# Linear attention beside a gated mixer, one core: a different tiling of the matrix M, and new places for den and r

## The chip, the cores and the metric

The kernel runs on one core of a Trainium2 chip. Times are device microseconds (us) of whole executions. A profiled execution also has a span, from its first to its last instruction, which is about 2 us shorter than the time.

The engines are named as in the profile: PE is TensorE's matmuls, PEld its weight loads, DVE VectorE, ACT ScalarE, POOL GpSimd, SP the sync engine that issues the DMAs. A `q` after a name is the engine's own instruction queue.

## The reference

The input is `x` of 2048 x 640 (bf16). Two branches are mixed by a gate per row.

```python
# A: linear attention, 32 heads of 20
q, k, v = split(x @ wqkv)                      # each [32, 2048, 20]
pq, pk = phi(q), phi(k)                        # phi(t) = (t+1 if t>0 else exp(t)) + 1e-6
kv  = einsum("hsd,hse->hde", pk, v)
z   = pk.sum(over s)
den = einsum("hqd,hd->hq", pq, z) + 1e-6
a   = (einsum("hqd,hde->hqe", pq, kv) / den) @ wo
# B: mixer
h  = gelu(layernorm(x) @ w1);  hs = shift_rows_of_four_column_groups(h) @ w2
x1 = x + hs
b  = x1 + gelu(layernorm(x1) @ w3) @ w4
out = g * a + (1 - g) * b                      # g = sigmoid((x * gate_w).sum(-1))
```

The kernel uses three rearrangements. It forms G = pk^T x first and then kv = G wv, so that v is never formed. It folds the block-diagonal kv into `wo` as one 640 x 640 matrix M, so that the attention branch is (pq / den) M. The reciprocals r = 1/den are spread over the features by four small matmuls (`r_unit`) and multiplied into pq (`scale_t`). The feature axis of q, k and M is stored in five chunks `j` of 128 rows, each row being (head, part i of 4).

## The kernel before

Only the parts that the change and the argument touch are shown; `pair()` hands out one of four PSUM buffers of two banks each, which is all of PSUM.

```python
    ps = ctx.enter_context(tc.tile_pool(name="ps", bufs=4, space=PSUM))
    def pair():
        return ps.tile([P, 2, 512], F32, name="pp")
    ...
    def den_mm():                       # four column groups of 32, one per tile of 512 rows
        pt = pair()
        for j in range(DC):
            for t in range(NT):
                nc.tensor.matmul(pt[32*t:32*(t+1), 0, :], lhsT=zbd[:, j, :], rhs=pqT[:, j, t*TS:(t+1)*TS], ...)
    def den_evac(pt):
        nc.scalar.activation(pt[:, 1, :], pt[:, 0, :], ACT.Copy, bias=1e-6)
        nc.vector.reciprocal(r_bf[:], pt[:, 1, :])
    def r_unit():                       # four row groups of 32
        pts = [pair(), pair()]
        for t in range(NT):
            nc.tensor.matmul(pts[t//2][:, t%2, :], lhsT=emat[32*t:32*(t+1), :], rhs=r_bf[32*t:32*(t+1), :], ...)
        for k in range(2):
            nc.scalar.copy(rb[:, 2*k:2*k+2, :], pts[k][:])
    ...
    def kv_unit():                      # six groups of up to 6 heads: 25 matmuls of 120 columns, 5 of 40
        ...                             # then 8 masked copies on DVE into kvT
    def m_unit(j):                      # 2 halves x 2 parts x 4 column groups
        pt = pair()
        for hf in range(2):
            for p in range(2):
                for q in range(4):
                    g = pairs_qg[2*q + p][1]
                    nc.tensor.matmul(pt[32*q:32*(q+1), hf, 0:HD], lhsT=kvT[:, 2*q + p, j, :],
                                     rhs=wo_sb[:, g, hf*HD:(hf+1)*HD], start=(p == 0), stop=(p == 1))
        nc.scalar.copy(m_sb[:, j, :].rearrange("p (h e) -> p h e", h=2), pt[:, :, 0:HD])
    ...
    for fcs in w1_split: w1_unit(0, fcs)        # W1 of tile 0, in three units: (0,1), (2,3), (4,)
    kv_unit()
    den_evac(den_mm())
    for cc in range(CPT): ln1_apply(3*CPT + cc)
    for fcs in w1_split: w1_unit(1, fcs)        # W1 of tile 1
    for j in range(DC): m_unit(j)
    r_unit()
    # then W2 of tile 0, W1 of tiles 2 and 3, and per tile W3, attention, W4
```

Of the kernel before, what the change touches and what calls it, by code (L numbers as in the profile page):

```python
# [7 lines left out]
ACT = mybir.ActivationFunctionType  # L8
# [8 lines left out]
def kernel(  # L17
# [14 lines left out]
    P = 128  # L32
# [12 lines left out]
    CG = D // 4  # L45
    shifts = [1, -1, 2, -2]
    YMAX = 60.0
    GH = 6
    GW = GH * Dh
    NG = 6  # L50
    row0 = [g * GW for g in range(5)] + [D - P]
    head0 = [g * GH for g in range(6)]
    heads = [min(GH, H - h) for h in head0]

    x2 = A_x.rearrange("b s d -> (b s) d")
    out2 = out.rearrange("b s d -> (b s) d")
# [12 lines left out]
    def pair():  # L69
        return ps.tile([P, 2, 512], F32, name="pp")  # L70
# [6 lines left out]
    w1x = const.tile([P, DC, P], BF16)  # L77
    w2_sb = const.tile([P, DC, D], BF16)
    w3_sb = const.tile([P, DC, F], BF16)
    wo_sb = const.tile([P, NG, D], BF16)  # L80
    m_sb = const.tile([P, DC, D], BF16)
    pairs_qg = [(0, 0), (0, 1), (1, 1), (1, 2), (2, 2), (2, 3), (3, 4), (3, 5)]
    kvT = const.tile([P, len(pairs_qg), DC, 32], BF16)
    rb = const.tile([P, NT, TS], BF16)
    r_bf = const.tile([P, TS], BF16)
    ident = const.tile([P, P], BF16)
# [2 lines left out]
    hmask = const.tile([P, H], F32)  # L89
    zbd = const.tile([P, DC, H], BF16)  # L90
    emat = const.tile([P, P], BF16)
    bmask = const.tile([P, GH * 4], F32)
    bmask5 = const.tile([P, 8], F32)
    ylog = const.tile([P, NCH], F32)
    gate = const.tile([P, NCH], F32)
    omg = const.tile([P, NCH], F32)
# [11 lines left out]
    gT = wk_sb  # L108
    xT = st1.tile([P, DC, S], BF16)
    pk = st1.tile([P, NCH, D], BF16)  # L110
    gs = st1.tile([P, 2, D], BF16)
    e_p = s1.enter_context(tc.tile_pool(name="e_p", bufs=3))

# [23 lines left out]
    load_x(8, 12)  # L137
    load_x(12, 16)
    sp.dma_start(wv_sb[:], wqkv_v[:, :, 2 * D:3 * D])
    sp.dma_start(w1_sb[:], B_w1.rearrange("(c p) f -> p c f", p=P))  # L140
    for g in range(NG):
        sp.dma_start(wo_sb[:, g, :], A_wo[row0[g]:row0[g] + P, :])
    for g in range(4):
        sp.dma_start(w2_sb[:, g, :], B_w2[CG * g:CG * g + P, :])
        sp.dma_start(w2_sb[32 * g:32 * (g + 1), 4, :], B_w2[CG * g + P:CG * (g + 1), :])
# [14 lines left out]
    for t in range(4):  # L160
# [2 lines left out]
                                base=0, pattern=[[1, P]], channel_multiplier=-4)  # L163
        nc.gpsimd.affine_select(out=sl, in_=sl, compare_op=ALU.is_ge, fill=0.0,
                                base=3, pattern=[[-1, P]], channel_multiplier=4)
    for m, n, off in ((bmask, GH, 0), (bmask5, 2, 88)):
        nc.gpsimd.memset(m[:], 1.0)
        nc.gpsimd.affine_select(out=m[:], in_=m[:], compare_op=ALU.is_ge, fill=0.0,
                                base=-off, pattern=[[-Dh, n], [0, 4]], channel_multiplier=1)
        nc.gpsimd.affine_select(out=m[:], in_=m[:], compare_op=ALU.is_ge, fill=0.0,  # L170
                                base=off + Dh - 1, pattern=[[Dh, n], [0, 4]], channel_multiplier=-1)
    nc.gpsimd.memset(kvT[:], 0.0)
    for g in range(4):
        nc.gpsimd.tensor_copy(w1x[:, :, 32 * g:32 * (g + 1)], w1_sb[:, :, CG * g + P:CG * (g + 1)])

# [24 lines left out]
    def warmup(n, w=TS):  # L200
        for i in range(n):
            nc.tensor.matmul(warm[:, 1, 0:w], lhsT=one[:, 0:P], rhs=one[:, 0:w], start=True, stop=True)

    warmup(6)
    warmup(3, P)
    kp = pair()
    turns = [(pair()[:, 0, :].bitcast(BF16), a, b) for a, b in ((0, 2), (2, DC))]
    tg = warm[:, 0, :].bitcast(BF16)
    for n, (ptb, a, b) in enumerate(turns):
# [3 lines left out]
        if n == 0:  # L213
            nc.tensor.transpose(tg[:, 0:DC], g5[:], ident[0:DC, 0:DC])
            nc.vector.tensor_copy(wk_sb[:, :, D], tg[:, 0:DC])
    warmup(3, P)
    for dc in range(DC):
        k_mm(kp, 0, (dc,))
        if dc < DC - 1:
# [23 lines left out]
    def den_mm():  # L243
# [3 lines that stand above are left out]
                nc.tensor.matmul(pt[32 * t:32 * (t + 1), 0, :], lhsT=zbd[:, j, :], rhs=pqT[:, j, t * TS:(t + 1) * TS],  # L247
                                 start=(j == 0), stop=(j == DC - 1))
        return pt

    def den_evac(pt):
        nc.scalar.activation(pt[:, 1, :], pt[:, 0, :], ACT.Copy, bias=1e-6)
        with nc.allow_low_precision(reason="rounded after a float32 division, as a copy would"):
            nc.vector.reciprocal(r_bf[:], pt[:, 1, :])

    def r_unit():
        pts = [pair(), pair()]
        for t in range(NT):
            nc.tensor.matmul(pts[t // 2][:, t % 2, :], lhsT=emat[32 * t:32 * (t + 1), :],
                             rhs=r_bf[32 * t:32 * (t + 1), :], start=True, stop=True)  # L260
        for k in range(2):
            nc.scalar.copy(rb[:, 2 * k:2 * k + 2, :], pts[k][:])

    def scale_t(t):
        sl = pqT[:, :, t * TS:(t + 1) * TS]
        nc.vector.tensor_tensor(sl, sl, rb[:, t:t + 1, :].broadcast_to([P, DC, TS]), op=ALU.mult)
# [69 lines left out]
    def w1_unit(t, fcs):  # L336
        pt = pair()
        for i, fc in enumerate(fcs):
            for dc in range(DC):
                w = w1_sb[:, dc, CG * fc:CG * fc + P] if fc < 4 else w1x[:, dc, :]  # L340
                nc.tensor.matmul(pt[:, i, :], lhsT=w, rhs=lnxT[t][:, dc, :], start=(dc == 0), stop=(dc == DC - 1))  # L341
        for i, fc in enumerate(fcs):
            if fc < 4:
                o = 2 + shifts[fc] + t * TS
                nc.scalar.activation(hsT[:, fc, o:o + TS], pt[:, i, :], ACT.Gelu_apprx_tanh)
            else:
                hx = hx_p.tile([P, TS], BF16, name="hx")
                nc.scalar.activation(hx[:], pt[:, i, :], ACT.Gelu_apprx_tanh)
                for g in range(4):
                    o = 2 + shifts[g] + t * TS  # L350
                    nc.vector.tensor_copy(hsT[32 * g:32 * (g + 1), 4, o:o + TS], hx[32 * g:32 * (g + 1), :])
# [2 lines left out]

    def kv_unit():
        pt = pair()
        for g in range(NG):
            n = heads[g] * Dh
            for fc in range(DC):
                nc.tensor.matmul(pt[:, g // 3, (g % 3) * GW:(g % 3) * GW + n], lhsT=wv_sb[:, fc, row0[g]:row0[g] + P],  # L360
                                 rhs=gT[:, fc, 0:D].rearrange("p (j h i) -> p j h i", j=DC, h=H)
                                 [:, :, head0[g]:head0[g] + heads[g], :], start=(fc == 0), stop=(fc == DC - 1))
        for b, (q, g) in enumerate(pairs_qg):
            h0, h1 = max(8 * q, head0[g]), min(8 * q + 8, head0[g] + heads[g])
            a0, a1 = h0 - head0[g], h1 - head0[g]
            m = bmask5 if g == 5 else bmask
            base = (g % 3) * GW
            nc.vector.tensor_tensor(
                kvT[:, b, :, 4 * (h0 - 8 * q):4 * (h1 - 8 * q)],
                pt[:, g // 3, base:base + heads[g] * Dh].rearrange("p (j a) -> p j a", j=DC)[:, :, 4 * a0:4 * a1],  # L370
                m[:, 4 * a0:4 * a1].unsqueeze(1).broadcast_to([P, DC, 4 * (a1 - a0)]), op=ALU.mult)

    def m_unit(j):
        pt = pair()
        for hf in range(2):
            for p in range(2):
                for q in range(4):
                    g = pairs_qg[2 * q + p][1]
                    nc.tensor.matmul(pt[32 * q:32 * (q + 1), hf, 0:HD], lhsT=kvT[:, 2 * q + p, j, :],  # L379
                                     rhs=wo_sb[:, g, hf * HD:(hf + 1) * HD], start=(p == 0), stop=(p == 1))  # L380
        nc.scalar.copy(m_sb[:, j, :].rearrange("p (h e) -> p h e", h=2), pt[:, :, 0:HD])  # L381

    nc.gpsimd.memset(hsT[:, :, 0:4], 0.0)
    nc.gpsimd.memset(hsT[:, :, S:S + 4], 0.0)
    for fcs in w1_split:
        w1_unit(0, fcs)
    kv_unit()
    den_evac(den_mm())
    for cc in range(CPT):
        ln1_apply(3 * CPT + cc)  # L390
    for fcs in w1_split:
        w1_unit(1, fcs)
    s1.close()
    w4p = ctx.enter_context(tc.tile_pool(name="w4p", bufs=1))
    w4_sb = w4p.tile([P, FF + 1, D], BF16)
# [1 line left out]
    x1p = ctx.enter_context(tc.tile_pool(name="x1p", bufs=8))  # L397
    st = {}

    for j in range(DC):  # L400
        m_unit(j)
    r_unit()


    def w2_unit(t, cc):
        c = t * CPT + cc
        if cc == 0:
            st[t] = dict(x1=[], mv=small.tile([P, CPT, 2], F32, name="mv2"))
        pt = pair()
        for hf in range(2):  # L410
            for fc in range(DC):
                nc.tensor.matmul(pt[:, hf, 0:HD], lhsT=hsT[:, fc, 2 + c * P:2 + (c + 1) * P],  # L412
                                 rhs=w2_sb[:, fc, hf * HD:(hf + 1) * HD], start=(fc == 0), stop=(fc == DC - 1))
        x1 = x1p.tile([P, D], F32, name="x1")
        nc.vector.tensor_tensor(x1[:].rearrange("p (h e) -> p h e", h=2), pt[:, :, 0:HD],  # L415
                                x_sb[:, c, 0:D].rearrange("p (h e) -> p h e", h=2), op=ALU.add)
        ln_stats(st[t]["mv"][:, cc, :], x1[:], small.tile([P, 2, 6], F32, name="bnst")[:])
        st[t]["x1"].append(x1)

    def ln2_rstd(t, c0, c1):  # L420
        if c0 == 0:
            st[t]["rstd"] = small.tile([P, CPT], F32, name="rstd2")
        rsqrt(st[t]["rstd"][:, c0:c1], st[t]["mv"][:, c0:c1, 1])
# [102 lines left out]

    for cc in range(CPT):
        w2_unit(0, cc)
        ln2_rstd(0, cc, cc + 1)
        if cc >= 1:  # L530
            ln2_apply(0, cc - 1)
# [4 lines left out]
    nc.sync.dma_start(w4_sb[:, 0:FF, :], B_w4[0:FF * P, :].rearrange("(c p) f -> p c f", p=P))  # L536
    nc.sync.dma_start(w4_sb[0:FR, FF, :], B_w4[FF * P:F, :])
    nc.sync.dma_start(w4_sb[FR:P, FF, :], B_w4[FF * P:F, :])
    scale_t(0)
    scale_t(1)  # L540
    for fcs in w1_split:
# [48 lines left out]
```

## Time and profile before

| | before |
|---|---|
| time, median of 3 first runs (range) | 266.99 us (266.32 to 267.23) |
| span of the profiled run | 265.1 us |
| PE busy | 259.4 us, 98% of the span |
| granted TensorE clock (1 is full speed) | 0.997 |

Two lines from the head of the page of the kernel before: the span, then per engine the busy microseconds, their share of the span and the number of instructions.

```profile
span 265.1 us, 4244 instructions
PE 259.4 (98%) x1728; PEld 162.0 (61%) x1744; DVE 139.3 (53%) x270; ACT 84.2 (32%) x122; POOL 20.3 (8%) x55
```

PE hardly ever stops, so what shortens PE's work or one of its few waits shortens the kernel. The stretch that the change rebuilds is best read from the chain of waits (start, length, engine, tile, line of the kernel, number of instructions). L360 is kv, L247 den, L379 M, L381 the copies of M out of PSUM, L412 W2, L459 W3. W1 (tile 1 between den and M, tiles 2 and 3 between W2 and W3) is left out.

```profile
1.78 3.93 DMA wk_sb<-in_A_wqkv_dram
...
76.73 1.43 PE pp L360 x30
78.16 1.19 PE pp L247 x20
...
84.86 0.69 PE pp L379 x16
85.56 2.49 ACT m_sb L381 x4
88.10 5.59 PE pp L412 x40
...
104.48 0.22 PE pp L459
```

From kv's start (76.73) to W3's start (104.48) takes 27.75 us. I use this stretch, "kv to W3", throughout: no DMA from outside starts or ends it. W2 waits for four ScalarE copies of M. The timeline of the kernel before shows how tightly:

```profile
84.78 2.90 PE L379 MATMUL pp<-wo_sb,kvT 128*32 128x320 bf16 x80
85.56 3.08 ACT L381 CAST m_sb<-pp 128x640 bf16<-128x640 f32 x5
87.62 0.40 PE L259 MATMUL pp<-r_bf,emat 32*128 32x512 bf16 x4
87.94 5.41 PEld L412 LDWEIGHTS <-hsT 128*128 128x128 bf16 x40 [0.23 <-issue]
88.10 5.59 PE L412 MATMUL pp<-w_sb,hsT 128*128 128x320 bf16 x40
```

M keeps PE to about 87.6 and r to about 87.9. W2's weights are in at 87.94, but its first matmul needs a PSUM pair that the fourth copy frees, and starts at 88.10. So at most 0.16 us of PE is lost there. The reciprocal, 3.36 us on DVE from 80.07 on, runs beside W1 and costs nothing.

### The profile page before, as it was taken

Reading aid. Unit: us, or ns where it says so; the run is one execution under the profiler, and the core shown is the slowest. Engines: PE = TensorE matmul, PEld = TensorE weight load, DVE = VectorE, ACT = ScalarE, POOL = GpSimd, SP = SyncE. Lnnn points to the kernel's source line nnn. Section 1 sums busy time; section 2 is a strip of 40 time slices with the busy share of each in tenths; the row PEclk is TensorE's granted clock in tenths of the full one; section 3 lists DMA queues with packets and bytes.
Section 4 is the critical chain, followed back from the end, with each engine's and each line's share of the span. In section 5 each row is a group of like instructions: output and inputs, shape, how many; then the busy total and the mean of one; then the engine's idle time right before and its main releaser. Section 6 shows DMA issues by size and latency. Waiting matters only on the chain.

```text
span 265.1 us, 4244 instructions
## 1 busy us (share of the span) xinstructions
PE 259.4 (98%) x1728; PEld 162.0 (61%) x1744; DVE 139.3 (53%) x270; ACT 84.2 (32%) x122; POOL 20.3 (8%) x55
## 2 busy tenths in 40 slices
PE   8999999999999999999999999999999999999994
PEld 4667555788755644565666556567556567455662
DVE  1688688899858588955422364512464503122032
ACT  1555544321165636522510313430212340333100
POOL 7100010012300140001000001000001000000000
PEclk9999999999999999999999999999999999999998
DMA  7999987015663527500132000132000042000011
GB/s 195 181 212 370 377 242 298 0 40 122 127 97 64 78 51 193 205 0 2 29 70 77 25 0 2 21 78 77 25 0 2 1 99 77 25 0 2 0 62 37
DMA packets 46092, 23.61 MB, mean 89 GB/s; under 512 B 35450, under 2 KB 45434, under 8 KB 46074
## 3 DMA queue, kind: packets, MB, share of 16 engines
q1 hardware_dynamic: 45632, 22.86, 33.2%
q10 hardware_dynamic: 442, 0.49, 0.5%
q8 instruction: 13, 0.21, 0.4%
q14 instruction: 5, 0.04, 0.1%
HBM read 12.21 MB, written 2.62 MB: 56 GB/s over the span
## 4 chain that ended last, share of the span: by engine, by line
PE 95%; DMA 1%; ACT 1%; issue 0%; ACTq 0%; DVE 0%
PE pp L476 22%; PE pp L459 21%; PE pp L307 8%; PE pp L412 8%; PE pp L443 8%; PE pp L190 8%; PE pp L341 8%; PE pp L232 8%; DMA wk_sb<-in_A_wqkv_dram 1%; PE pp L464 1%; PE pp L485 1%; ACT m_sb L381 1%; PE pp L360 1%; PE pp L247 0%; PE pp L379 0%
## 5 line engine op out<-in xcount | busy, mean ns | idle before, releaser
L467 ACT ACTIVATE h<-pp 128x1024 bf16<-128x1024 f32 (+1 forms) x28 | 27.8, 992 | 102.8 <-PE pp L459 94.4
L459 PE MATMUL pp<-lnxT,w_sb 128*128 128x512 bf16 x249 | 59.8, 379 | 0.6
L476 PE MATMUL pp<-w_sb,h 128*128 128x320 bf16 x416 | 57.9, 299 | 0.0
L476 PEld LDWEIGHTS <-h 128*128 128x128 bf16 x416 | 40.0, 98 | 17.0 <-issue 1.9
L459 PEld LDWEIGHTS <-w_sb 128*128 128x128 bf16 x260 | 25.4, 98 | 26.7
L492 DVE SCALAR_TENSOR_TENSOR oc<-pp,omg,x 128x640 bf16<-128x640 f32 x15 | 12.9, 882 | 44.1 <-PE pp L485 27.1
L446 DVE SCALAR_TENSOR_TENSOR x<-pp,gate,x 128x640 f32<-128x640 f32 x16 | 13.9, 868 | 29.4 <-PE pp L443 29.4
L415 DVE TENSOR_TENSOR x<-pp,x_sb 128x640 f32<-128x640 f32 x16 | 13.1, 820 | 22.6 <-PE pp L412 22.6
L182 ACT ACTIVATE e<-pp 128x640 bf16<-128x640 f32 (+1 forms) x26 | 21.5, 826 | 9.6 <-PE pp L232 9.6
L443 PE MATMUL pp<-m_sb,pqT 128*128 128x320 bf16 x160 | 24.3, 299 | 0.0
L412 PE MATMUL pp<-w_sb,hsT 128*128 128x320 bf16 x160 | 23.9, 299 | 0.1
L190 PE MATMUL pp<-wk_sb,xT 128*128 128x320 bf16 (+1 forms) x160 | 22.7, 300 | 0.1
L307 PE MATMUL pp<-x_sb,pk 128*128 128x320 bf16 (+1 forms) x160 | 22.3, 300 | 0.0
L232 PE MATMUL pp<-xT,hsT 128*128 128x512 bf16 x98 | 21.6, 379 | 0.1
L307 PEld LDWEIGHTS <-pk 128*128 128x128 bf16 x160 | 18.8, 117 | 3.5
L412 PEld LDWEIGHTS <-hsT 128*128 128x128 bf16 x160 | 15.6, 98 | 8.2 <-issue 0.2
L443 PEld LDWEIGHTS <-pqT 128*128 128x128 bf16 x160 | 15.7, 98 | 7.7
L190 PEld LDWEIGHTS <-xT 128*128 128x128 bf16 x160 | 15.4, 98 | 6.6 <-DMA xT<-in_A_x_dram 0.6
L341 PE MATMUL pp<-lnxT,w_sb 128*128 128x512 bf16 x77 | 17.8, 379 | 0.2
L232 PEld LDWEIGHTS <-hsT 128*128 128x128 bf16 x100 | 11.8, 118 | 9.7
L277 POOL TENSOR_SCALAR rstd<-mv 128x4 f32<-128x4 f32 (+1 forms) x11 | 3.4, 312 | 156.5 <-DVE mv L283 156.5
L184 DVE SCALAR_TENSOR_TENSOR pk<-pp,e 128x640 bf16<-128x640 f32 x16 | 13.2, 824 | 1.7
(76 smaller groups left out, 189.7 us busy)
## 6 DMA issues: line engine op xcount, KB each, us to landing
out_dram<-oc SPq DMA_DIRECT2D x15, 160.0 KB, 1.8
w_sb<-in_B_w_dram SPq DMA_DIRECT2D x1, 2160.0 KB, 8.4
w_sb<-in_B_w_dram SPq DMA_DIRECT2D x1, 2080.0 KB, 10.2
x_sb<-in_A_x_dram SPq DMA_DIRECT2D x2, 640.0 KB, 10.0
x_sb<-in_A_x_dram SPq DMA_DIRECT2D x1, 1120.0 KB, 7.5
wo_sb<-in_A_wo_dram SPq DMA_DIRECT2D x6, 160.0 KB, 7.7
hsT<-in_A_wqkv_dram SPq DMA_DIRECT2D x1, 800.0 KB, 5.0
m_sb<-in_A_wqkv_dram SPq DMA_DIRECT2D x1, 800.0 KB, 11.1
```

The lines of the kernel that those rows point to most:

```text
L182: nc.scalar.activation(ev, src, ACT.Exp)
L184: nc.vector.scalar_tensor_tensor(dst, src, 0.0, ev, op0=ALU.max, op1=ALU.add)
L190: nc.tensor.matmul(pt[:, hf, 0:n], lhsT=xT[:, dc, c * P:(c + 1) * P], rhs=wk_sb[:, dc, hf * HD:hf * HD + n], start=(dc == 0), stop=(dc == ...
L232: nc.tensor.matmul(pt[:, t % 2, :], lhsT=wq_sb[:, dc, :].rearrange("p (m j) -> p j m", j=DC)[:, j], rhs=xT[:, dc, t * TS:(t + 1) * TS], st ...
L307: nc.tensor.matmul(pt[:, hf, 0:HD + hf], lhsT=w, rhs=x_sb[:, c, hf * HD:(hf + 1) * HD + hf], start=(c == 0), stop=(c == NCH - 1))
L341: nc.tensor.matmul(pt[:, i, :], lhsT=w, rhs=lnxT[t][:, dc, :], start=(dc == 0), stop=(dc == DC - 1))
L412: nc.tensor.matmul(pt[:, hf, 0:HD], lhsT=hsT[:, fc, 2 + c * P:2 + (c + 1) * P], rhs=w2_sb[:, fc, hf * HD:(hf + 1) * HD], start=(fc == 0), ...
L443: nc.tensor.matmul(pt[:, hf, 0:HD], lhsT=pqT[:, j, c * P:(c + 1) * P], rhs=m_sb[:, j, hf * HD:(hf + 1) * HD], start=(j == 0), stop=(j == D ...
L446: nc.vector.scalar_tensor_tensor(x1, pt[:, :, 0:HD], gate[:, c:c + 1], x1, op0=ALU.mult, op1=ALU.add)
L459: nc.tensor.matmul(pt[:, k, :], lhsT=w3_sb[:, dc, fc * P:(fc + 1) * P], rhs=lnT[:, dc, :], start=(dc == 0), stop=(dc == DC - 1))
L467: nc.scalar.activation(h2[:, 2 * i * TS:2 * i * TS + n], pt[:].rearrange("p h e -> p (h e)")[:, 0:n], ACT.Gelu_apprx_tanh)
L476: nc.tensor.matmul(dst, lhsT=st[t]["h2"][:, fc * TS + cc * P:fc * TS + (cc + 1) * P], rhs=w4_sb[:, fc, a:b], start=start and fc == 0, stop ...
```

## The change

The intent is to use fewer array passes for M. Each quarter of the 640 features (160 rows of `wo`, 8 heads) is cut into 128 rows and a rest of 32. The 128 go through K=128 matmuls (`kvA`, `woA`; K is the number of rows that a matmul sums over). The rests of 32 go through 32x32 tiles (`kvB`, `woB`), arranged so that for each j the four quarters lie in four different row groups, and all sixteen (j = 0..3, quarter q) can run at once. For j=4 the rests are zero-padded to K=128 (`kvZ`). den moves from behind kv to just before M; r moves from behind M to behind W1 of tile 2. The diff, cut to its core:

```diff
     def kv_unit():
-        # 6 groups: 25 matmuls of 120 columns, 5 of 40; 8 masked copies
+        # 4 quarters x 5 of 140 columns, 5 more of 160; then
+        for q in range(4):
+            nc.vector.tensor_tensor(kvA[:, q, :, 0:4*NA], dst[q]..., maskA..., op=ALU.mult)
+        for q in range(4):
+            rows = slice(32*q, 32*(q+1))
+            for j in range(DC):
+                r = (q + j) % 4
+                out = kvB[32*r:32*(r+1), j, 4*(HQ-NB):] if j < 4 else kvZ[rows, q, 4*(HQ-NB):]
+                nc.vector.tensor_tensor(out, bv[rows, j, q, :], maskB[rows, :], op=ALU.mult)   # 20 small ones
-    def m_unit(j): ...
+    m_cols = ((0, TS), (TS, D))                      # 512 + 128 columns
+    def m_a(j, pt, start, stop):
+        for hf, (a, b) in enumerate(m_cols):
+            for q in range(4):
+                nc.tensor.matmul(pt[32*q:32*(q+1), hf, 0:b-a], lhsT=kvA[:, q, j, :], rhs=woA[:, q, a:b], ...)
+    def m_all():
+        pts = [pair() for _ in range(4)]
+        for hf, (a, b) in enumerate(m_cols):
+            for j in range(4):
+                for q in range(4):
+                    r = (q + j) % 4
+                    rows = slice(32*r, 32*(r+1))
+                    nc.tensor.matmul(pts[j][32*q:32*(q+1), hf, 0:b-a], lhsT=kvB[rows, j, :],
+                                     rhs=woB[rows, j, a:b], start=True, stop=False)
+        for j in range(4):
+            m_a(j, pts[j], False, True)
+            m_evac(j, pts[j])
+        pt = pair()
+        m_a(4, pt, True, False)
+        ...                                          # 8 matmuls with kvZ, then m_evac(4, pt)
@@ order of the work
     kv_unit()
-    den_evac(den_mm())
     ...
     for fcs in w1_split: w1_unit(1, fcs)
+    dp = den_mm()
+    nc.scalar.activation(den_sb[:], dp[:, 0, :], ACT.Copy, bias=1e-6)
-    for j in range(DC): m_unit(j)
-    r_unit()
+    m_all()
+    den_recip(0, 3)                                  # the last quarter follows inside W2
@@ after W1 of tile 2
+    r_unit()
     scale_t(0)
```

Three things come along with it. The weights need other copies: 24 DMAs where there were 6. The masks need eight more GpSimd instructions. The two groups of three 128-column warm-up matmuls became one of 384 columns each.

More of the change, by code (lines that the diff above doesn't have):

```diff
@@ L47 @@
     YMAX = 60.0
-    GH = 6
-    GW = GH * Dh
-    NG = 6
-    row0 = [g * GW for g in range(5)] + [D - P]
-    head0 = [g * GH for g in range(6)]
-    heads = [min(GH, H - h) for h in head0]
+    HQ = H // 4
+    EQ = HQ * Dh
+    NA = 7
+    NB = 2
     x2 = A_x.rearrange("b s d -> (b s) d")
@@ L79 @@
     w3_sb = const.tile([P, DC, F], BF16)
-    wo_sb = const.tile([P, NG, D], BF16)
+    woA = const.tile([P, 4, D], BF16)
+    woB = const.tile([P, 4, D], BF16)
     m_sb = const.tile([P, DC, D], BF16)
-    pairs_qg = [(0, 0), (0, 1), (1, 1), (1, 2), (2, 2), (2, 3), (3, 4), (3, 5)]
-    kvT = const.tile([P, len(pairs_qg), DC, 32], BF16)
+    kvA = const.tile([P, 4, DC, 32], BF16)
+    kvB = const.tile([P, 4, 32], BF16)
+    kvZ = const.tile([P, 4, 32], BF16)
+    den_sb = const.tile([P, TS], F32)
     rb = const.tile([P, NT, TS], BF16)
@@ L91 @@
     emat = const.tile([P, P], BF16)
-    bmask = const.tile([P, GH * 4], F32)
-    bmask5 = const.tile([P, 8], F32)
+    maskA = const.tile([P, NA * 4], F32)
+    maskB = const.tile([P, NB * 4], F32)
     ylog = const.tile([P, NCH], F32)
@@ L110 @@
     pk = st1.tile([P, NCH, D], BF16)
+    wvB = st1.tile([P, DC, P], BF16)
     gs = st1.tile([P, 2, D], BF16)
@@ L139 @@
     sp.dma_start(wv_sb[:], wqkv_v[:, :, 2 * D:3 * D])
+    for q in range(4):
+        sp.dma_start(wvB[:, :, 32 * q:32 * (q + 1)], wqkv_v[:, :, 2 * D + q * EQ + P:2 * D + (q + 1) * EQ])
     sp.dma_start(w1_sb[:], B_w1.rearrange("(c p) f -> p c f", p=P))
-    for g in range(NG):
-        sp.dma_start(wo_sb[:, g, :], A_wo[row0[g]:row0[g] + P, :])
+    for q in range(4):
+        sp.dma_start(woA[:, q, :], A_wo[q * EQ:q * EQ + P, :])
+        for k in range(4):
+            r = (q + k) % 4
+            sp.dma_start(woB[32 * r:32 * (r + 1), k, :], A_wo[q * EQ + P:(q + 1) * EQ, :])
     for g in range(4):
@@ L165 @@
                                 base=3, pattern=[[-1, P]], channel_multiplier=4)
-    for m, n, off in ((bmask, GH, 0), (bmask5, 2, 88)):
-        nc.gpsimd.memset(m[:], 1.0)
-        nc.gpsimd.affine_select(out=m[:], in_=m[:], compare_op=ALU.is_ge, fill=0.0,
-                                base=-off, pattern=[[-Dh, n], [0, 4]], channel_multiplier=1)
-        nc.gpsimd.affine_select(out=m[:], in_=m[:], compare_op=ALU.is_ge, fill=0.0,
-                                base=off + Dh - 1, pattern=[[Dh, n], [0, 4]], channel_multiplier=-1)
-    nc.gpsimd.memset(kvT[:], 0.0)
+    nc.gpsimd.memset(maskA[:], 1.0)
+    nc.gpsimd.affine_select(out=maskA[:], in_=maskA[:], compare_op=ALU.is_ge, fill=0.0,
+                            base=0, pattern=[[-Dh, NA], [0, 4]], channel_multiplier=1)
+    nc.gpsimd.affine_select(out=maskA[:], in_=maskA[:], compare_op=ALU.is_ge, fill=0.0,
+                            base=Dh - 1, pattern=[[Dh, NA], [0, 4]], channel_multiplier=-1)
+    nc.gpsimd.memset(maskB[:], 1.0)
+    for q in range(4):
+        sl = maskB[32 * q:32 * (q + 1), :]
+        nc.gpsimd.affine_select(out=sl, in_=sl, compare_op=ALU.is_ge, fill=0.0,
+                                base=P - 6 * Dh, pattern=[[-Dh, NB], [0, 4]], channel_multiplier=1)
+        nc.gpsimd.affine_select(out=sl, in_=sl, compare_op=ALU.is_ge, fill=0.0,
+                                base=7 * Dh - 1 - P, pattern=[[Dh, NB], [0, 4]], channel_multiplier=-1)
+    for m in (kvA, kvB, kvZ):
+        nc.gpsimd.memset(m[:], 0.0)
     for g in range(4):
@@ L204 @@
     warmup(6)
-    warmup(3, P)
+    warmup(1, 3 * P)
     kp = pair()
@@ L215 @@
             nc.vector.tensor_copy(wk_sb[:, :, D], tg[:, 0:DC])
-    warmup(3, P)
+    warmup(1, 3 * P)
     for dc in range(DC):
@@ L249, in den_mm, with den_recip @@
         return pt
-    def den_evac(pt):
-        nc.scalar.activation(pt[:, 1, :], pt[:, 0, :], ACT.Copy, bias=1e-6)
+    def den_recip(k0, k1):
+        sl = slice(k0 * P, k1 * P)
         with nc.allow_low_precision(reason="rounded after a float32 division, as a copy would"):
-            nc.vector.reciprocal(r_bf[:], pt[:, 1, :])
+            nc.vector.reciprocal(r_bf[:, sl], den_sb[:, sl])
     def r_unit():
@@ L356, in kv_unit @@
         pt = pair()
-        for g in range(NG):
-            n = heads[g] * Dh
-            for fc in range(DC):
-                nc.tensor.matmul(pt[:, g // 3, (g % 3) * GW:(g % 3) * GW + n], lhsT=wv_sb[:, fc, row0[g]:row0[g] + P],
-                                 rhs=gT[:, fc, 0:D].rearrange("p (j h i) -> p j h i", j=DC, h=H)
-                                 [:, :, head0[g]:head0[g] + heads[g], :], start=(fc == 0), stop=(fc == DC - 1))
-        for b, (q, g) in enumerate(pairs_qg):
-            h0, h1 = max(8 * q, head0[g]), min(8 * q + 8, head0[g] + heads[g])
-            a0, a1 = h0 - head0[g], h1 - head0[g]
-            m = bmask5 if g == 5 else bmask
-            base = (g % 3) * GW
-            nc.vector.tensor_tensor(
-                kvT[:, b, :, 4 * (h0 - 8 * q):4 * (h1 - 8 * q)],
-                pt[:, g // 3, base:base + heads[g] * Dh].rearrange("p (j a) -> p j a", j=DC)[:, :, 4 * a0:4 * a1],
-                m[:, 4 * a0:4 * a1].unsqueeze(1).broadcast_to([P, DC, 4 * (a1 - a0)]), op=ALU.mult)
@@ L373, in m_unit @@
-    def m_unit(j):
-        pt = pair()
-        for hf in range(2):
-            for p in range(2):
-                for q in range(4):
-                    g = pairs_qg[2 * q + p][1]
-                    nc.tensor.matmul(pt[32 * q:32 * (q + 1), hf, 0:HD], lhsT=kvT[:, 2 * q + p, j, :],
-                                     rhs=wo_sb[:, g, hf * HD:(hf + 1) * HD], start=(p == 0), stop=(p == 1))
-        nc.scalar.copy(m_sb[:, j, :].rearrange("p (h e) -> p h e", h=2), pt[:, :, 0:HD])
+        gv = gT[:, :, 0:D].rearrange("p c (j h i) -> p c j h i", j=DC, h=H)
@@ new lines, in kv_unit @@
+        na, nb = NA * Dh, 4 * NB * Dh
+        dst = [pt[:, 0, q * na:(q + 1) * na] for q in range(3)] + [pt[:, 1, 0:na]]
+        dstB = pt[:, 1, na:na + nb]
+        for q in range(4):
+            for fc in range(DC):
+                nc.tensor.matmul(dst[q], lhsT=wv_sb[:, fc, q * EQ:q * EQ + P],
+                                 rhs=gv[:, fc, :, q * HQ:q * HQ + NA, :], start=(fc == 0), stop=(fc == DC - 1))
+        for fc in range(DC):
+            nc.tensor.matmul(dstB, lhsT=wvB[:, fc, :],
+                             rhs=gT[:, fc, 0:D].rearrange("p (j q r) -> p j q r", j=DC, q=4)[:, :, :, 4 * (HQ - NB):],
+                             start=(fc == 0), stop=(fc == DC - 1))
@@ new lines, in kv_unit @@
+        for q in range(4):
+            nc.vector.tensor_tensor(kvA[:, q, :, 0:4 * NA], dst[q].rearrange("p (j a) -> p j a", j=DC),
+                                    maskA[:].unsqueeze(1).broadcast_to([P, DC, 4 * NA]), op=ALU.mult)
+        bv = dstB.rearrange("p (j q r) -> p j q r", j=DC, q=4)
+        for q in range(4):
+            rows = slice(32 * q, 32 * (q + 1))
+            for j in range(DC):
+                r = (q + j) % 4
+                out = kvB[32 * r:32 * (r + 1), j, 4 * (HQ - NB):] if j < 4 else kvZ[rows, q, 4 * (HQ - NB):]
+                nc.vector.tensor_tensor(out, bv[rows, j, q, :], maskB[rows, :], op=ALU.mult)
@@ new lines @@
+    m_cols = ((0, TS), (TS, D))
+    def m_a(j, pt, start, stop):
+        for hf, (a, b) in enumerate(m_cols):
+            for q in range(4):
+                nc.tensor.matmul(pt[32 * q:32 * (q + 1), hf, 0:b - a], lhsT=kvA[:, q, j, :], rhs=woA[:, q, a:b],
+                                 start=start, stop=stop)
+    def m_all():
+        pts = [pair() for _ in range(4)]
+        for hf, (a, b) in enumerate(m_cols):
+            for j in range(4):
+                for q in range(4):
+                    r = (q + j) % 4
+                    rows = slice(32 * r, 32 * (r + 1))
+                    nc.tensor.matmul(pts[j][32 * q:32 * (q + 1), hf, 0:b - a], lhsT=kvB[rows, j, :],
+                                     rhs=woB[rows, j, a:b], start=True, stop=False)
+        for j in range(4):
+            m_a(j, pts[j], False, True)
+            m_evac(j, pts[j])
+        pt = pair()
+        m_a(4, pt, True, False)
+        for hf, (a, b) in enumerate(m_cols):
+            for q in range(4):
+                nc.tensor.matmul(pt[32 * q:32 * (q + 1), hf, 0:b - a], lhsT=kvZ[:, q, :], rhs=woB[:, 0, a:b],
+                                 start=False, stop=True)
+        m_evac(4, pt)
@@ L383, with m_evac @@
+    def m_evac(j, pt):
+        nc.scalar.copy(m_sb[:, j, :], pt[:].rearrange("p h e -> p (h e)")[:, 0:D])
     nc.gpsimd.memset(hsT[:, :, 0:4], 0.0)
@@ L398 @@
     st = {}
-    for j in range(DC):
-        m_unit(j)
-    r_unit()
+    m_all()
+    den_recip(0, 3)
     def w2_unit(t, cc):
@@ L528 @@
         w2_unit(0, cc)
+        if cc == 1:
+            den_recip(3, 4)
         ln2_rstd(0, cc, cc + 1)
```

## The prediction

> **What bounds it now.** TensorE. The page shows PE busy 259.4 of 265.1 us (98%) at full granted clock, and 95% of the chain of waits is PE. Between G and W2 of tile 0, the stretch that the change rebuilds, the chain reads: kv 1.43 us (30 matmuls), den 1.19, W1 of tile 1 5.5, then M, r and a wait, 84.8 to 88.1. In the timeline M's 80 matmuls of 32 columns stream from 84.78 to about 87.6 (34 ns each, so four column groups do run at once), r takes 0.3 more, and W2 loads its weights at 87.94 but starts at 88.10: the chain puts four ScalarE copies of M (0.62 each, 2.5 us) before it, so the copies, which must free a PSUM pair, end last by only 0.16 us. DVE's 3.36 us reciprocal at 80.1 is hidden.
>
> **What the change costs, worked out from these.**
> - kv: 25 matmuls of 120 columns (52 ns) plus 5 of 40 (25 ns) become 20 of 140 (about 61) plus 5 of 160 (69): 1.43 -> 1.56, +0.13 us.
> - den: same 20 matmuls, moved: 0.
> - M: columns streamed through four groups fall from 5x2x640 to 6x640 plus the sixteen 32x32 tiles. Ideal: M's 2.8 us -> 6x0.27 for the K=128 parts and Z, plus 0.3 to 1.0 for the tiles. The matmul count stays 80, and the 128-wide ones will be bound by issue, about 25 ns each, not by streaming (the 40-column kv matmuls show about 25). I expect 2.2 to 2.7 us of PE work.
> - A new wait: M now takes all four PSUM pairs at once, and the fourth is den's, freed by a 0.58 us ScalarE copy that starts only when den ends. Tiles of j=3 wait for it, some 0.3 to 0.6 us.
> - r leaves the stretch, with its two 1 us copies, but costs PE about 0.35 us behind W1 of tile 2, with two changes of tiling mode. The Trainium skill, "TensorEngine Tiling (Array Packing)", Key Properties, says that changing the mode drains the engine; den here takes 1.19 us against 20x512 columns/4 = 1.08 at W1's rate of 0.216 per 512, which agrees with 0.1 us per change.
> - ScalarE still needs two M copies before W2 may start, about 1.3 us after the first M block; no longer last, or equal.
> - DVE: the reciprocal is cut, 2.5 us behind den (before W2's first add needs DVE) and 0.84 us between W2's adds; W3 waits for transposes that have about 1.7 us of slack. Twenty more small masks in kv and 19 more weight DMAs, 60 to 25 us before use: hidden.
>
> **Sum.** Den and M to W2's start: 1.19+3.3 -> 1.19 + about 2.9; kv +0.13; r +0.35. Net about -0.1 us, within noise.
>
> **Predicted:** 266.8 us, range 265.8 to 267.9. Faster by over 2%: 0.01; within 2%: 0.96; slower: 0.03.
>
> **Signs.** Right: den start to W2 start 3.9 to 4.5 us (before, den 1.2 plus M to W2 3.3); a PE gap of 0.3 to 0.6 before the fourth tile group, released by den's ScalarE copy; r 0.3 to 0.4 us between W1 of tiles 2 and 3; W3 not waiting longer for transposes; everything after W3 of tile 0 unchanged.
>
> **What would make it wrong.** The same page, Gotcha 1, says that different row tiles cannot access one PSUM bank at once. Here the four tiles of one j sit in one bank, in different quadrants. If that serialises, 16x0.216+16x0.055 = 4.3 us, the kernel is 3 to 3.5 us slower. If the tiles pack perfectly and den's copy hides, it gains 0.6 to 1.0 us. The 16-byte runs of kv's new right side could stream slowly (+0.3). Delayed adds on DVE could hold W3 back.

## The result, and the profile after

| | before | after |
|---|---|---|
| median (range), 6 runs each | 267.11 us (266.32 to 267.86) | 266.81 us (266.3 to 267.05) |
| ratio, 95% interval | | 0.9989, 0.997 to 1.0009 |
| span of the profiled run | 265.1 us | 265.3 us |
| kv to W3, from the chain | 27.75 us | 27.97 us |
| W3's start to the end of the span | 160.6 us | 159.9 us |

A ratio is the mean time of one kernel's fast runs over that of the other's of the same rounds, so it is not quite the ratio of the medians.

The chain of waits of the changed kernel. L377 and L380 are kv, L355 W1, L261 den, L435 the copy of den out of PSUM, L409 the 32x32 tiles, L399 the K=128 parts of M, L418 the zero-padded rest, L454 W2, L273 r, L501 W3:

```profile
1.78 4.74 DMA wk_sb<-in_A_wqkv_dram
...
77.44 1.22 PE pp L377 x20
78.66 0.35 PE pp L380 x5
79.00 5.40 PE pp L355 x25
84.40 1.22 PE pp L261 x20
...
85.64 0.61 ACT den_sb L435
...
86.29 0.45 PE pp L409 x16
86.74 1.64 PE pp L399 x40
88.38 0.27 PE pp L418 x8
88.65 5.54 PE pp L454 x40
94.19 5.40 PE pp L355 x25
99.58 0.33 PE pp L273 x4
...
105.41 2.16 PE pp L501 x10
```

Set beside the chain before, stage by stage: kv 1.43 -> 1.57 us; W1 of tile 1 from the end of the unit in front 5.51 -> 5.40; den's start to W2's start 1.19 + 3.24 = 4.43 -> 88.65 - 84.40 = 4.25; W2 5.59 -> 5.54; W1 of tiles 2 and 3 with what lies between them 10.79 -> 11.22. The sum is +0.14 - 0.11 - 0.18 - 0.05 + 0.43 = +0.23, which is the 27.97 against 27.75 but for rounding. So **the stretch that was meant to get shorter got longer by 0.22 us**.

The whole kernel is nevertheless not slower. On the chain its K matmuls start 0.8 us later in this profiled run, because the first weights landed later (DMA, 4.74 against 3.93 us). I take that for chance: in the traces below kv starts anywhere from 76.73 to 77.33 us with the old M and from 76.97 to 77.44 with the new. At the other end, W3's start to the end of the span got 0.7 us shorter, although nothing in that part of the program was changed. Two questions follow. What held M back? And where do the 0.7 us at the end come from?

The timeline of the changed kernel around M (the bracket is the idle time before, and what ended it):

```profile
85.52 0.42 PE L409 MATMUL pp<-woB,kvB 32*32 32x512 bf16 x12
85.64 0.60 ACT L435 ACTIVATE den_sb<-pp 128x512 f32<-128x512 f32 x1 [0.61 <-PE pp L261]
86.29 0.45 PE L409 MATMUL pp<-woB,kvB 32*32 32x512 bf16 x20 [0.35 <-ACT den_sb L435]
87.18 3.08 ACT L423 CAST m_sb<-pp 128x640 bf16<-128x640 f32 x5 [0.94 <-PE pp L399]
88.19 0.46 PE L418 MATMUL pp<-woB,kvZ 128*32 128x512 bf16 x8
```

Twelve tiles (j=0..2) start at 85.52, and the rest only at 86.29, when ScalarE has copied den out of the fourth PSUM pair. The chain counts 0.65 us from den's end (85.64) to there; the first twelve tiles run inside it, so PE itself is idle for 0.35. The tiles themselves pack as the change hoped. The windows view of the changed kernel, for those instructions alone (window, its length, PE busy and in parentheses how many were running, then clock and DMA):

```profile
85.52:85.54 0.02, 0.02 (x6) 1.00 0.37 77
85.54:85.56 0.02, 0.02 (x12) 1.00 0.54 90
```

Twelve tiles of 512 columns, in three banks, are all running within 0.04 us. Had the four of one bank run one after the other, they would need 0.2 us each. The ends of matmuls are modelled in a profile, so the chain is the firmer sign: the last twenty tiles, four of them of 512 columns in one bank, took 0.45 us until the next group, where those four alone would need 4 x 0.216 = 0.86 one after the other. The danger named in the prediction did not happen.

### The profile page after: what moved, and what is told of

It reads as the page before. It is cut to its first block, busy times and chain, and to the rows that moved or that the text cites. A ratio compares the mean times of both kernels' runs of the same rounds, so it can differ in the third digit from the quotient of the medians.

```text
span 265.3 us, 4284 instructions
## 1 busy us (share of the span) xinstructions
PE 261.0 (98%) x1735; PEld 161.3 (61%) x1735; DVE 142.4 (54%) x287; ACT 84.2 (32%) x122; POOL 21.1 (8%) x63
## 4 chain that ended last, share of the span: by engine, by line
PE 96%; DMA 2%; ACTq 0%; ACT 0%; DVE 0%; issue 0%
PE pp L518 22%; PE pp L501 21%; PE pp L321 8%; PE pp L454 8%; PE pp L485 8%; PE pp L355 8%; PE pp L246 8%; PE pp L204 8%; DMA wk_sb<-in_A_wqkv_dram 2%; PE pp L506 1%; PE pp L527 1%; PE pp L399 1%; PE pp L261 0%; PE pp L377 0%; ACT den_sb L435 0%; ACTq L129 0%
## 5 line engine op out<-in xcount | busy, mean ns | idle before, releaser
L501 PE MATMUL pp<-lnxT,w_sb 128*128 128x512 bf16 x260 | 60.4, 379 | 0.0
L501 PEld LDWEIGHTS <-w_sb 128*128 128x128 bf16 x260 | 25.4, 98 | 26.7
L454 PE MATMUL pp<-w_sb,hsT 128*128 128x320 bf16 x160 | 23.9, 299 | 0.0
L454 PEld LDWEIGHTS <-hsT 128*128 128x128 bf16 x160 | 15.6, 98 | 8.2 <-issue 0.3
L355 PE MATMUL pp<-lnxT,w_sb 128*128 128x512 bf16 x80 | 17.9, 379 | 0.0
L197 DVE TENSOR_SCALAR e<-e 128x640 bf16<-128x640 bf16 (+1 forms) x26 | 9.6, 370 | 8.9 <-ACT e L196 7.4
```

Source lines behind the costliest of these rows:

```text
L355: nc.tensor.matmul(pt[:, i, :], lhsT=w, rhs=lnxT[t][:, dc, :], start=(dc == 0), stop=(dc == DC - 1))
L454: nc.tensor.matmul(pt[:, hf, 0:HD], lhsT=hsT[:, fc, 2 + c * P:2 + (c + 1) * P], rhs=w2_sb[:, fc, hf * HD:(hf + 1) * HD], start=(fc == 0), ...
L501: nc.tensor.matmul(pt[:, k, :], lhsT=w3_sb[:, dc, fc * P:(fc + 1) * P], rhs=lnT[:, dc, :], start=(dc == 0), stop=(dc == DC - 1))
```

## The experiments

Theory A: the changed M costs less PE work, but takes all four PSUM pairs at once and so waits for copies; den's move is harmless, and r's move costs 0.43 us. Rivals are named with each run. All outputs are right.

### The moves alone

Edit: the kernel before, with den and r where the changed kernel has them, and the old kv and M.

```diff
     kv_unit()
-    den_evac(den_mm())
     ...
+    dp = den_mm(); nc.scalar.activation(den_sb[:], dp[:, 0, :], ACT.Copy, bias=1e-6)
     for j in range(DC): m_unit(j)
-    r_unit()
+    den_recip(0, 3)
     ...                                  # den_recip(3, 4) inside W2; r_unit() behind W1 of tile 2
```

> Kernel before, with only den moved next to M and r moved behind W1 of tile 2; M and kv keep their old form. Theory A (the move of r costs PE 0.4 us in its new place, the old M has no wait for four PSUM pairs at once): den's start to W2's start is 1.2 + 2.8 = 4.0 us against 4.4 in the kernel before and 4.25 in the changed kernel; no PE gap inside M; r costs 0.43 between W1 of tiles 2 and 3; start of kv to start of W3 27.6 us (before 27.75, changed 27.97). Rival B (the new M is what gains and the moves are free or lose nothing): this kernel is as slow as the one before, 27.75 or more, and slower than the changed one.

The chain of this run (L248 den, L380 M, L414 W2):

```profile
84.06 1.19 PE pp L248 x20
85.25 2.72 PE pp L380 x80
87.97 5.54 PE pp L414 x40
```

Den's start to W2's start took 3.91 us, M ran without a gap, and kv to W3 took 27.50 us (77.23 to 104.73): 0.25 less than before and 0.47 less than the changed kernel. Theory A holds. **In this stretch the moves were the good half of the change, the new M the bad half.** Old M issues one j at a time and needs one free pair at a time, so den's copy hides behind the first j; W2 shows no wait for a copy, probably because r's two pairs no longer lie between. By stage against the kernel before: W1 of tile 1 -0.11 (den no longer stands in front of it, so one change of tiling mode falls away), den's start to W2's start -0.52, W2 -0.05, and W1 of tiles 2 and 3 with r between them +0.43.

The same kernel was timed later:

> The same kernel as the run that only moved den and r, timed. Its traced stretch from kv to W3 is 0.25 us shorter than before. If that is all that differs, the ratio to the kernel before is 0.999, inside an interval of about 0.2% on either side.

Median 266.8 us over 6 runs, before 267.17 over 11; ratio 0.9991, interval 0.9977 to 1.0005, as expected. The stretch was 27.51 us (76.88 to 104.39), so it repeats to 0.01.

### The new M alone

Edit: the changed kernel with den (and its old copy and reciprocal, both inside PSUM) back behind kv and r back behind M.

> The changed kernel with den back behind kv and r back behind M; only kv and M keep their new form. Theory A (M takes four PSUM pairs at once, so the last unit before it must be copied out first, whichever it is): the gap before the tiles of j=3 stays, now for the copy of W1's last unit, 0.5 to 0.7 us; W2 then waits for four ScalarE copies that start later than before, so W1's end to W2's start is 3.8 to 4.0 us (before 3.24), and kv to W3 is 28.4 to 28.7 us. Rival B (the gap is den's own, and goes with it): no gap, W1's end to W2's start at most 3.3, kv to W3 about 27.8.

The timeline of this run (L267 the reciprocal, L408 the tiles; the first eight tiles, at 85.25, are left out):

```profile
83.43 3.36 DVE L267 RECIPROCAL r_bf<-pp 128x512 bf16<-128x512 f32 x1
...
86.84 0.46 PE L408 MATMUL pp<-woB,kvB 32*32 32x512 bf16 x24 [1.03 <-DVE r_bf L267]
```

My expectation was too low, and named the wrong copy. kv to W3 took 29.59 us (77.07 to 106.66), 1.8 more than before. The gap stands at j=2, not j=3, and is 1.0 us; it waits for den's pair, which in this order is held until the reciprocal has read it. The reciprocal starts at 83.43, where the kernel before had it at 80.07, because DVE first works through the new kv's 24 masked copies, 79.07 to 83.40; the old eight took 1.27 us. The rival is half refuted: the gap did not go when den moved away, but it is still den's pair that is waited for, so theory A's "whichever it is" is not shown either. The run also shows how the two halves of the change hang together: behind the small masks, a den that keeps its pair until the reciprocal has read it becomes costly. Den in its old place, but copied out to SBUF at once, was not tried.

### Is the narrow part of M bound by issue?

Edit: M's columns as 320 + 320.

```diff
-    m_cols = ((0, TS), (TS, D))
+    m_cols = ((0, HD), (HD, D))
```

> The changed kernel with M's columns cut 320+320 in place of 512+128. Theory A (the 128-column matmuls of M are bound by issue at about 25 ns each, not by streaming): the forty K=128 matmuls of j=0..4 fall from 1.64 to about 1.36 us, Z from 0.27-0.3 to 0.27, den's start to W2's start from 4.25 to 3.9, kv to W3 from 27.97 to 27.65. Rival B (streaming binds, 640 columns either way): no change within 0.05 us.

The chain of this run, the K=128 parts of M:

```profile
86.27 1.64 PE pp L399 x40
```

Theory A's form fails here and its rival holds: 1.64 us again, and kv to W3 27.98 (76.97 to 104.95). The total alone would not settle it, since a later wait could swallow the gain. But ScalarE's first copy of M, which needs only the first group, starts 0.44 us after the K=128 parts in both kernels (86.74 to 87.18; here 86.27 to 86.71). Four column groups of 128 columns stream side by side as well as wide ones. My figure of 25 ns came from kv's 40-column matmuls, which use the full array one after another, and does not carry over to column tiles. The 1.64 us must hold something else: five groups of 640 columns are 5 x 0.27 = 1.35 at the rate of the sixth (0.27 for L418), and a change of tiling mode is 0.1. The 0.2 left is probably the fifth group's wait for a pair, which the first copy of M frees: that copy starts at 87.18 in the changed kernel and takes about 0.7, and the fifth group starts at about 87.9 instead of 87.75. The run after next supports this.

### Work in the gap

Edit: M of j=4 first, on a pair that has long been free; tiles for j=0..2 only; j=3 last, made like j=4.

```diff
     def m_all():
-        pts = [pair() for _ in range(4)]
+        m_z(4)                            # K=128 part, zero-padded rest, copy
+        pts = [pair() for _ in range(3)]
         ... tiles for j in range(3), then m_a and m_evac for j in range(3)
+        m_z(3)
```

> The changed kernel with M of j=4 (two K=128 parts) first, on a pair that is long free, tiles for j=0..2 only, and j=3 made like j=4, last. Theory A (the gap is the wait for den's pair, and work that needs no such pair fills it): the gap before the tiles goes from 0.65 us to under 0.1; the tiles cost 0.35, Z twice 0.3; den's start to W2's start 4.25 -> 3.8 to 3.95, kv to W3 27.97 -> 27.5 to 27.7. Rival B (the gap comes from the change of tiling mode or from the tiles' own writes to shared banks): the gap stays where the tiles begin, and the time grows by the extra Z part, 0.3.

Den's start to W2's start was 88.07 - 84.25 = 3.82 us, and kv to W3 27.54 (77.29 to 104.83), as theory A expected; the mode-change rival, which wanted the time to grow, is out. The gap was not gone entirely: the tiles took 0.61 us instead of 0.35, because j=2 now used den's pair, and den's copy ended at 86.10 while the tiles began at 85.92.

### The K=128 parts ahead of the tiles

Edit: as the last one, with `m_a` of j=0..2 before their tiles, so that den's pair is wanted 0.5 us later still.

```diff
         pts = [pair() for _ in range(3)]
+        for j in range(3):
+            m_a(j, pts[j], True, False)
         ... tiles, now start=False, stop=True
```

> As the run that put j=4 first, but with the K=128 parts of j=0..2 ahead of their tiles, so that den's pair is wanted about 1.1 us after den ends, when its copy (0.65) is done. Theory A (the waits for copies are all that M's new form lost): no PE gap from den to W2; six 0.27 groups for j=4, 0, 1, 2 with Z of j=4, tiles 0.27 and two changes of mode, j=3 and its Z 0.54: den's start to W2's start 1.2 + 2.45 = 3.65 us (changed kernel 4.25, old M after the same moves 3.91); kv to W3 27.3 to 27.45 (27.97; 27.50). Time against the kernel before: 0.3 to 0.45 us less, 0.998 to 0.999. Rival (W2 then waits for ScalarE's copies of j=0..2, which now all start after the tiles): W2 starts 0.3 us or more later than M ends, 3.9 or more.

The chain of this run (L399 the K=128 parts of j=0..2, L412 the tiles, L428 the first copy of M, L459 W2; j=3, which runs beside that copy, is not on the chain):

```profile
85.87 0.81 PE pp L399 x24
86.69 0.45 PE pp L412 x24
...
87.17 0.70 ACT m_sb L428
...
87.91 5.59 PE pp L459 x40
```

The three K=128 groups now take 0.81 us, 0.27 each, where five took 1.64 before: with no pair to wait for, the extra 0.2 is gone. Tiles and two mode changes come to 0.45. But the rival was also partly right: W2 waited 0.16 us for the first copy of M, which can start only when the tiles are done. Den's start to W2's start was 3.77 us (expected 3.65), kv to W3 27.55 (77.18 to 104.73), no better than the old M's 27.50. **Even with the wait for den's pair and that of the fifth group taken away, the new M gains nothing over the old one in this place**: what M saves in array passes goes to kv (+0.14) and to one wait or another.

The time was a surprise: median 266.21 us over 6 runs against 267.17, ratio 0.9968, interval 0.9954 to 0.9982. That is 0.85 us, and only 0.20 lies in the stretch. The rest pointed to the end of the kernel.

### Den's copy twice, and r twice

Edits: in the changed kernel, the ScalarE copy of den issued twice; and, separately, `r_unit`'s four matmuls issued twice in a row.

> The changed kernel with ScalarE's copy of den issued twice. Theory A (the tiles of j=3 wait for that copy and everything after waits with them): the gap grows by 0.55 to 0.6 us, den's start to W2's start from 4.25 to 4.8, and kv to W3 from 27.97 to 28.55. Rival (a later wait, for the copies of M or for DVE, hides it): under 0.2 more.

The timeline of this run, the tiles behind the wait:

```profile
86.53 0.45 PE L409 MATMUL pp<-woB,kvB 32*32 32x512 bf16 x20 [0.98 <-ACT den_sb L436]
```

The idle time before the tiles of j=3 grew from 0.35 to 0.98 us, den to W2 from 4.25 to 4.88, and kv to W3 from 27.97 to 28.60 (77.05 to 105.65). All of the added 0.63 arrives in the kernel: the copy is on the critical path.

> The changed kernel with the four matmuls of r issued twice in a row into the same PSUM. If r's cost of 0.43 us in its new place is 0.22 of streaming and 0.2 for two changes of tiling mode, the second four add 0.22: W1 of tile 2 to W3's start 11.44 against 11.22 in the changed kernel. If each of the four costs its own 0.1 us (no packing of row tiles), they add 0.4 or more.

The chain of this run, r:

```profile
99.19 0.54 PE pp L273 x8
```

Eight matmuls take 0.54 us where four took 0.33, and kv to W3 grew by 0.22 to 28.19 (77.05 to 105.24). So four row groups stream at once, in 0.22 us, and the other 0.2 of r's 0.43 comes once for each visit, at its two borders. I put it down to the two changes of tiling mode. Borders without such a change bear this out: W1 of tile 1 straight behind kv took 25 x 0.216 = 5.40 us, behind den 5.51, and the old M straight behind den 2.72 where its columns alone need 2.70. Before, r lay behind M and needed only one change more, and part of it hid in W2's wait for a copy.

### The end of the kernel

In every trace so far with the old M, W3's start to the end of the span took 160.6 us, and in every one with the new M 159.9 to 160.0. The difference lies wholly behind the last DVE instruction. Everything after it belongs to the closing line of the program (L585 before, L630 after): the sync engine waits for the last DMAs, all engines meet, GpSimd clears the semaphores, all meet again. Two answers from the view of that line, in 0.05 us windows, first of the kernel before (duration min/median/max in ns, then the starts):

```profile
L585 POOLq EVENT_SEMAPHORE_RANGE_CLEAR  x1: 96/96/96, 264.2 to 264.2; - x1
L585 POOLq DRAIN  x1: 181/181/181, 264.7 to 264.7; - x1
```

and then of the changed kernel:

```profile
L630 POOLq EVENT_SEMAPHORE_RANGE_CLEAR  x1: 96/96/96, 265.0 to 265.0; - x1
L630 POOLq DRAIN  x1: 34/34/34, 265.1 to 265.1; - x1
```

Before, GpSimd stands still for about 0.35 us between two neighbouring instructions, and the second takes 181 ns; after, it follows at once in 34 ns. The waits of the sync engine show the same, and a second difference, in its wait for the DMAs (what waited, for what: us in total, times, longest). Before:

```profile
SPq L585 <- DMA out_dram<-oc: 1.3, 1, 1.3
SPq L585 <- PEq L585: 1.1, 2, 0.9
```

and after:

```profile
SPq L630 <- DMA out_dram<-oc: 1.1, 1, 1.1
SPq L630 <- PEq L630: 0.6, 2, 0.4
```

In the windows, the sync engine's seven semaphore waits stood in one row before, the first ending at 263.5 when the last output had landed and six following at 47 ns each. In the changed kernel three pass at once and the late one is the fourth. I also read in the built programs that with 18 more DMAs the last output uses another of the DMA semaphores (the sixth instead of the fourth). So the theory is that eight GpSimd instructions and 18 DMAs, which came along with the change, shortened the end by shifting where things fall. To test it, I gave the kernel before each of the two effects alone, and nothing else of the change. First the eight instructions:

```diff
+    for _ in range(8):
+        nc.gpsimd.memset(spare[:], 0.0)
```

> The kernel before with nothing but eight more tiny memsets on GpSimd early on (the changed kernel has eight more GpSimd instructions). In every trace so far with the old M the span ends 3.2 to 3.3 us after the last DVE instruction, in every one with the new M 2.5; 0.5 of that lies on GpSimd, between its range clear of the semaphores and its next drain (0.36 us against none, and the drain 181 against 34 ns). Theory T (this depends only on where GpSimd's program ends): the gap goes, the tail is 2.7 to 2.8, the stretch from kv to W3 stays 27.75, and the time falls by 0.5 us, ratio 0.998. Rival U (the short tail comes from the new form of kv and M): nothing changes, ratio 1.000.

The sync engine's waits in this run, at the closing line (now L588):

```profile
SPq L588 <- DMA out_dram<-oc: 1.3, 1, 1.3
SPq L588 <- PEq L588: 0.6, 2, 0.4
```

and GpSimd's drain there:

```profile
L588 POOLq DRAIN  x1: 34/34/34, 264.7 to 264.7; - x1
```

The gap is gone, and with it 0.5 us of the wait for the other engines, while the wait for the DMAs is as before. The end, from the last DVE instruction on, took 2.79 us (before 3.26). The stretch was unchanged at 27.76 (77.09 to 104.85), and the time fell: median 266.52 us over 5 runs against 267.15 over 9, ratio 0.9976, interval 0.996 to 0.9991. **Eight memsets that compute nothing took about as much off this kernel as the whole change did**: 0.47 us of the trace from kv's start on, against 0.7 - 0.22 = 0.5 for the change (the intervals of the times overlap). The rival, that the short end comes from the new kv and M, is out.

Then two small loads on the sync queue, which move the last output to the semaphore that it has in the changed kernel:

```diff
+    for k in range(2):
+        sp.dma_start(spare_g[:, k, :], gate_w.rearrange("(c p) -> c p", p=P))
```

> The kernel before with two more tiny loads on the sync queue, so that the last output's DMA has the same semaphore as in the changed kernel. There the late semaphore is the fourth of the seven that the sync engine waits for at the end, before it is the first, with six more waits of 47 ns behind it. Theory T: three of the seven waits pass before the last output lands, and the tail is 0.14 us shorter (3.26 to about 3.1), with GpSimd's gap unchanged. Rival U: the order of waits stays, and the tail too.

The same waits with two more loads in place of the memsets:

```profile
SPq L588 <- DMA out_dram<-oc: 1.1, 1, 1.1
SPq L588 <- PEq L588: 1.1, 2, 0.9
```

The wait for the DMAs went to that of the changed kernel and GpSimd's gap stayed; the end, from the last DVE instruction to the end of the span, was 3.15 us against 3.26. The stretch was 27.75 (76.84 to 104.59). This is 0.1 us, read from the trace alone; a single time could not show it.

### The parts that help, together

Edit: the kernel that only moves den and r, with both pads.

> The kernel that only moves den and r (old kv and M), with both pads. If the parts add up: stretch from kv to W3 27.5, tail 2.5 to 2.6, so 0.25 + 0.65 = 0.9 us less than before, ratio 0.9966; equal to the best version so far (0.9968) without any of the new M. If the pads do nothing, 0.999 as before.

Median 265.94 us over 5 runs against 267.15 over 9, ratio 0.9957, interval 0.9943 to 0.9972. The stretch was 27.51 (77.33 to 104.84), W3 to the end 160.0. The traces account for 0.25 + 0.65 = 0.9 us; the timed 1.15 has this inside its interval. This is the fastest kernel, and it has the old M. Against the one with the reordered new M (0.9968) the intervals overlap, so I do not call it faster than that one.

| kernel | kv to W3 | W3 to end of span | time against before |
|---|---|---|---|
| before | 27.75 | 160.6 | 1 |
| changed | 27.97 | 159.9 | 0.9989 (0.997 to 1.0009) |
| moves alone | 27.50, 27.51 | 160.6, 160.6 | 0.9991 (0.9977 to 1.0005) |
| new M alone | 29.59 | 159.9 | one run, 268.31 us |
| changed, 320 + 320 columns | 27.98 | 160.0 | one run, 266.6 us |
| changed, j=4 first | 27.54 | 160.0 | one run, 266.49 us |
| changed, K=128 parts first | 27.55 | 160.0 | 0.9968 (0.9954 to 0.9982) |
| before, GpSimd pad | 27.76 | 160.2 | 0.9976 (0.996 to 0.9991) |
| before, DMA pad | 27.75 | 160.5 | one run, 266.91 us |
| moves and both pads | 27.51 | 160.0 | 0.9957 (0.9943 to 0.9972) |

The one-run times had 266.86 us (first three, one run) and 267.15 (the DMA pad, median of 9) beside them. The first run of the moves alone took 267.05 beside the same 266.86; the runs with den's copy and with r doubled, 267.31 and 266.9, had 267.17 (median of 11).

## Why the prediction was right or wrong

The predicted time, 266.8 us in 265.8 to 267.9, "within 2%", was met: 266.81. But the sum behind it was not right. It put the whole effect, -0.1 us, into the stretch; there it was +0.22. There is also a slip in it: its own terms, -0.4, +0.13 and +0.35, add up to +0.08. The same three measured -0.18, +0.14 and +0.43; W1 of tile 1 and W2, not in the sum, gave back 0.11 and 0.05. What brought the time to 266.81 came from the end of the kernel, -0.7, which the prediction did not mention. So the wait for den's copy was forecast rightly, but that the number fits this closely is luck: the net effect is made of a loss and a larger gain of which neither was forecast. Point by point:

- kv, "+0.13": measured 1.43 -> 1.57, +0.14. Right. The 16-byte runs streamed at full rate (five matmuls of 160 columns in 0.35 us).
- "den: moved: 0": 1.19 -> 1.22 us. Right.
- M, "2.2 to 2.7 us of PE work": from den's end to W2's start 3.03 us, less 0.65 for den's copy and about 0.2 for the fifth pair, is about 2.2 (or 2.5, if the first twelve tiles, which run inside the 0.65, are counted). In range, though for the wrong reason: "the 128-wide ones will be bound by issue, about 25 ns each" failed. The cut into 320 + 320 columns changed nothing; they stream.
- "Tiles of j=3 wait for it, some 0.3 to 0.6 us": the wait is there, for the copy named, and doubling the copy doubled it. It is 0.65 us on the chain, just above the range; PE's own idle time, which the signs name, is 0.35.
- Missed: the fifth group of M waits about 0.2 us for the first copy of M. "ScalarE still needs two M copies before W2 may start ... no longer last, or equal" was right about W2, but did not ask the same of M's own fifth pair.
- r, "about 0.35": 0.43, being 0.22 of streaming and 0.2 of two changes of tiling mode. The skill page's statement that a mode change drains the engine agrees with these 0.1 us each.
- "Den and M to W2's start: 1.19+3.3 -> 1.19 + about 2.9" is the term that was most mis-sized: a gain of 0.4 was forecast and 0.18 measured (4.43 -> 4.25, inside the sign's 3.9 to 4.5), for the two waits above.
- "If that serialises ... slower": it did not. Twelve tiles, four to a bank in four different row groups, in different quadrants, were running together within 0.04 us.
- "everything after W3 of tile 0 unchanged": unchanged as far as PE goes, but not the end. This step failed by more than the whole predicted effect.
- W3 did not wait for transposes, and DVE's cut reciprocal and the extra DMAs (18, not 19) stayed hidden. Right.

That eight more GpSimd instructions remove the gap is shown; why is not. The Trainium skill, "Runtime: NRT & Kernel Launch", Instruction fetch mechanics, says that an engine's instructions are fetched in blocks by a DMA queue of its own, so a program whose end falls at a block's edge could stall there; the page itself calls the cost of such an edge mostly hidden. It fits that the traces with the gap (before, moves alone, DMA pad) have an instruction-fetch packet on one queue, q14, at the very end, and that those without it have none there on that queue. But in the kernel before this packet lands near 265.4 us, after the gap and after the span, so it is not shown to be what GpSimd waited for.

## What to carry to other kernels

A unit that takes every PSUM buffer at once can turn a copy for what ran before it into a wait, so count, beside array passes, which buffer is wanted when, and who frees it; here about 0.5 us of saved passes (2.72 to about 2.2) met 0.85 us of waits. When a change is worth a few tenths of a microsecond, split the span into stretches that the trace repeats to 0.01 us, and look at the stretches that the change did not touch as well: instructions and DMAs that come along with it can move the end of the program by more than the change itself. A test that adds only those, with the real change left out, tells the two apart.

## What the Trainium skill lacked or had wrong

- "TensorEngine Tiling (Array Packing)", Gotcha 1, says that different row tiles cannot access the same PSUM bank simultaneously. It is too wide: four tiles of different row groups in one bank, but in different quadrants, ran together here (four tiles of 512 columns and sixteen of 128 in 0.45 us, where the four alone need 0.86 if serial). "PSUM — Partial Sum Buffer", Terms, has it finer, in its row on the quadrant: different quadrants of one bank may be accessed at the same time. It says this of different engines; this trace shows it for row tiles of TensorE. Different row groups in one bank and one quadrant were not tried.
- "TensorEngine Tiling (Array Packing)", Key Properties, says that a change of tiling mode drains the engine, but gives no time: about 0.1 us each here (r: 0.43 us in all, 0.22 of it streaming).
- No page says that the closing sequence of a program can change with instructions far ahead of it: the end of this kernel varied from 2.5 to 3.26 us, 0.5 us of it with eight GpSimd instructions and 0.1 us with two small loads.
